# Fused attention and mixing on one Trainium2 core: where P is transposed in the first attention from the seventh pair on

## The chip, the core and the metric

The kernel runs on one core of one Trainium2 chip. The metric is the device time of one execution in microseconds (us). The engines are named as the profile names them: PE (TensorE), DVE (VectorE), ACT (ScalarE), POOL (GpSimd) and SP (SyncE, which only issues transfers here). PEld is PE's loading of weights, which runs beside its matmuls.

## What is computed

Three layers follow each other on 8 sequences of 576 tokens, with a width of 512. The change touches the first.

```python
# first attention: 8 heads of 64, in chunks of 64 tokens
scores = scale * q_c @ k_c.transpose(0, 1, 2, 4, 3)
attn = np.exp(scores - scores.max(-1, keepdims=True))
attn = attn / (attn.sum(-1, keepdims=True) + 1e-09)
x = attn @ v_c
# mixing: x_prev is x one token earlier
xk = mu_k * x + (1 - mu_k) * x_prev
xr = mu_r * x + (1 - mu_r) * x_prev
x = sigmoid(xr @ w_r) * (np.maximum(xk @ w_k, 0) ** 2 @ w_v)
# then four gated experts of causal attention, not touched here
```

## The kernel before, in words

Tokens are cut into 36 tiles of 128, two chunks of 64 each. Two tiles make a pair (18 pairs, 0 to 17), three tiles make a unit of the mixing layer (12 units of 384 tokens). The projections of the mixing layer are done with each operand split into a high and a low part, so that each product is three matmuls of 128x128 by 384 columns (`mm3`, L91 to L97).

The first attention of a pair runs in named steps. `lq`, `lk`, `lv` load a tile's queries, keys and values from SP (`load_qk`, `load_v`). `Tq` and `Tk` transpose queries and keys. From tile 12 on (`by_dve`, that is from the seventh pair) DVE does this in blocks of 32x32 (`by_blocks`, L197): the loads of such tiles place the blocks so that the transpose of each block alone is enough, in 8 transfers of 32 KB per tensor and tile (L149 to L153). Before tile 12, PE transposes whole 128x128 squares against an identity into a PSUM bank (`to_bank`, L187), and ACT copies the bank out in `Eq` and `Ek` (`from_bank`, L192). `S` makes the scores with 64 matmuls of 64x64 (`s_scores`, L211 or L214), into PSUM. On DVE `X` takes maxima and `U` subtracts them, on ACT `E` is the exponential, on DVE `Z` sums and inverts and `Y` multiplies: the result is P. `Tp` transposes P of one tile, in all pairs with four PE transposes (L187), and `Ep` copies the bank to the tile PT on ACT (L192). `V` multiplies PT by the values with 64 matmuls (`s_products`, L267 or L270) and `W` copies the results to XT.

The mixing steps: `a`, `b`, `c`, `d` (with `k` or `r`) shift and split x on ACT, DVE, ACT, DVE; `r`, `k` and each half of `v` are twelve matmuls on PE; `s` is the sigmoid, `K` three ACT steps (L364 to L366), `J` the low part on DVE (L370); `y` multiplies on DVE (L387), `z` takes the high part on POOL (L84), `x` the low part on DVE (L396), and `D` stores from POOL's queue (L401). `prev` moves a column on POOL.

The order of all this is written out by hand as two lists of steps: START for the first two units, with pairs 0 to 5 done in it, and TWO_UNITS, which is run four times (units 2 to 9, each turn with the attention of three pairs ahead: pairs 6 to 17). `follow` (L495) issues the steps in the list's order, and `in_line` (L485) chains each instruction to the one before on its own engine, so that every engine keeps the list's order. In TWO_UNITS the numbers are offsets: `Tp0` is the first tile of the turn, `V-1` the products of the pair that the turn before left over. After the fourth turn `V17` and `W17` stand alone (L515); the last two units and the experts follow in an order that the compiler's scheduler makes.

Attention's PSUM banks are five (`pa`), the tiles PT have two buffers, the tag `cz` (128x512) two, the loads two each.

Of the kernel before, what the change touches and what calls it, by code (L numbers as in the profile page):

```python
# [8 lines left out]
F32 = mybir.dt.float32  # L9
# [34 lines left out]
CH = 64  # L44
UNIT = 384
TWO_UNITS = """
Tk0 Tk1 lk2 Tq0 k0,0 Tq1 k0,1 K0,0 lq2 J0,0 V-1 S0 K0,1 k0,2 W-1 X0 U0 prev1 k0,3 ar1,0 K0,2 br1,0 J0,1 k0,4 E0 J0,2
lq3 K0,3 k0,5 J0,3 K0,4 Z0 k0,6 K0,5 lv0 J0,4 Y0 k0,7 K0,6 J0,5 J0,6 Tp0 K0,7 v0,0,0 lv1 lk3 cr1,0 J0,7 ar1,1 Tk2 Tp1
v0,0,1 dr1,0 Tq2 v0,1,0 y0,0 br1,1 z0,0 cr1,1 x0,0 v0,1,1 ak1,0 dr1,1 D0,0 bk1,0 ar1,2 lk4 br1,2 v0,2,0 cr1,2 ck1,0
dr1,2 y0,1 ak1,1 v0,2,1 z0,1 bk1,1 dk1,0 ck1,1 x0,1 ar1,3 v0,3,0 D0,1 y0,2 br1,3 z0,2 cr1,3 v0,3,1 dr1,3 dk1,1 ak1,2  # L50
Ep0 r1,0 y0,3 x0,2 z0,3 Tk3 D0,2 r1,1 bk1,2 s1,0 lk5 ak1,3 r1,2 ck1,2 bk1,3 dk1,2 ck1,3 Tq3 s1,1 r1,3 s1,2 lq4 dk1,3
Ep1 V0 S1 k1,0 W0 X1 x0,3 s1,3 k1,1 U1 D0,3 K1,0 lq5 J1,0 k1,2 K1,1 E1 J1,1 k1,3 lv2 K1,2 k1,4 Z1 K1,3 Y1 k1,5 J1,2
lv3 Tq4 K1,4 Tp2 J1,3 lq6 k1,6 Ep2 J1,4 K1,5 Tk4 k1,7 Tk5 K1,6 J1,5 Tq5 lk6 Tp3 J1,6 v1,0,0 Ep3 K1,7 V1 S2 J1,7 v1,0,1
X2 W1 U2 prev2 v1,1,0 ar2,0 lk7 br2,0 ar2,1 y1,0 cr2,0 br2,1 v1,1,1 z1,0 dr2,0 cr2,1 ar2,2 dr2,1 ar2,3 v1,2,0 y1,1 lv4
x1,0 z1,1 lq7 br2,2 D1,0 v1,2,1 br2,3 cr2,2 E2 x1,1 dr2,2 v1,3,0 Z2 ak2,0 cr2,3 lv5 D1,1 Y2 v1,3,1 dr2,3 bk2,0 ak2,1
Tp4 y1,2 ck2,0 r2,0 Ep4 z1,2 y1,3 dk2,0 z1,3 x1,2 Tp5 s2,0 x1,3 D1,2 r2,1 bk2,1 Ep5 r2,2 ck2,1 ak2,2 dk2,1 s2,1 bk2,2
ak2,3 D1,3 r2,3 ck2,2 bk2,3 s2,2 dk2,2 ck2,3 dk2,3 s2,3
""".split()

FIRST_UNITS, FIRST_PAIRS = 2, 6  # L60
CFG = dict(ps=(2, 3, 1, 2), P=5, sm=3, load=5, lag=(3, 4), out=(5, 1), qk1=(1, 1), qk0=(9, 1.1), v=(10, 0.9), order=((3, 0), (2, 0), (0, 0), (4, 0), (1, 0), (3, 1), (2, 1), (0, 1), (1, 1)), after=1, conv='v', clo='v', chi='g', x2hi='g', x2lo='v', ylo='g', yhi='v', xt='aa', r2='av', klo='vv', amul='vv', nearly=2, x2b=1, yb=4, qb=4, direct=((0, 1), (1, 1), (1, 1)), tailAV=4, kp=2, yt=1, yf=2, zb=1, om=(3, 2, 1, 0, 4), hp=1000, x2d=2, early=(2, 1), dact=3, rate0=0.43, rate=0.45, sh=(10, 12, 2), sh2=(11, 1, -1), pro='cccqqaacavvcaaaaacaacaaaascc', alag=2, seq=0, end=2, outL=(11, 2), outE=2, kcp='aa', dsc='v', ldb=2, vb=2, cn=512, stb=2, xb=4, pa=5, tb=2, first_j=7, dve_j=6)
# [38 lines left out]
def attn_mix(tc, at, x2T, q, k, v, mu_k, mu_r, w_k, w_v, w_r, ident, attended_all, mixed_k):  # L100

    nc = tc.nc
    B, H, S, D = q.shape
    HP = H // 2
# [10 lines left out]
    with ExitStack() as ctx:  # L115
# [15 lines left out]
        qkv = {}  # L131

        def runs(t):
            b, s = divmod(t * 128, S)
            return [(0, b, s, 128)] if s + 128 <= S else [(0, b, s, CH), (CH, b + 1, 0, CH)]

        def by_dve(t):
            return t >= 2 * CFG["dve_j"]
# [21 lines left out]
                qkv[nm, t] = x  # L160

        def load_v(t):
            if by_dve(t):
                x = at.tile([128, H, D], F32, tag="ldv", bufs=CFG["vb"], name="ldv")
                for p, b, s, n in runs(t):
                    nc.sync.dma_start(out=x[p:p + n], in_=v[b, :, s:s + n, :].rearrange("h p d -> p h d"))
                qkv["v", t] = x
                return
            x = at.tile([128, 2, HP, D], F32, tag="ldv", bufs=CFG["vb"], name="ldv")
            for c in range(2):  # L170
                b, s = divmod(t * 128 + c * CH, S)
                for e in range(2):
                    r = e ^ c
                    nc.sync.dma_start(out=x[r * 64:(r + 1) * 64, c],
                                      in_=v[b, e::2, s:s + CH, :].rearrange("g p d -> p g d"))
            qkv["v", t] = x

        qT, kT, PP, PT, XT = {}, {}, {}, {}, {}
# [11 lines left out]
        def from_bank(p, nm):  # L190
            o = at.tile([128, HP, 128], F32, tag=nm, bufs=CFG["tb"], name=nm)
            nc.scalar.activation(out=o, in_=p, func=ACTF.Copy)  # L192
            return o
# [6 lines left out]
        def s_scores(j):  # L200
            banks = [bank("Sps").rearrange("p g (i k) -> p i g k", i=2) for _ in range(2)]
            for i in range(2):
                a, b = qT.pop(2 * j + i), kT.pop(2 * j + i)
                for g in range(HP):
                    for c in range(2):
                        for o in range(2):
                            e = o ^ c
                            r, cc = slice(e * 64, e * 64 + 64), slice(c * CH, (c + 1) * CH)
                            with tc.high_priority(1000) if j < CFG["first_j"] else nullcontext():
                                if by_dve(2 * j):  # L210
                                    nc.tensor.matmul(out=banks[e][cc, i, g], lhsT=a[r, g, c], rhs=b[r, g, c],  # L211
                                                     start=True, stop=True)
                                    continue
                                nc.tensor.matmul(out=banks[o][cc, i, g], lhsT=a[r, g, cc], rhs=b[r, g, cc],  # L214
                                                 start=True, stop=True)
            SB[j] = banks
# [38 lines left out]
        def s_products(j):  # L255
            VB[j] = banks = [bank("PVps").rearrange("p g (i k) -> p i g k", i=2) for _ in range(2)]
            for i in range(2):
                t = 2 * j + i
                a, vt = PT.pop(t), qkv.pop(("v", t))
                for g in range(HP):  # L260
                    for c in range(2):
                        for o in range(2):
                            e = o ^ c
                            r, cc = slice(o * 64, o * 64 + 64), slice(c * CH, (c + 1) * CH)
                            with tc.high_priority(1000) if j < CFG["first_j"] else nullcontext():
                                if by_dve(t):
                                    nc.tensor.matmul(out=banks[o][cc, i, g], lhsT=vt[r, 2 * g + c],  # L267
                                                     rhs=a[r, g, cc], start=True, stop=True)
                                    continue
                                nc.tensor.matmul(out=banks[c][e * 64:e * 64 + 64, i, g], lhsT=vt[r, c, g],  # L270
                                                 rhs=a[r, g, cc], start=True, stop=True)

# [110 lines left out]
        X2 = {}  # L383
# [25 lines left out]
        n = CFG["cn"]  # L409
# [45 lines left out]
        def to_T(d, nm):  # L455
            def f(t):
                x = PP.pop(t).rearrange("p g o k -> p (g o k)") if nm == "PT" else qkv.pop((nm[0], t))
                if nm != "PT" and by_dve(t):
                    d[t] = by_blocks(x, nm)
                else:  # L460
                    TB[nm, t] = to_bank(x)
            return f

        def from_T(d, nm):
            def f(t):
                d[t] = from_bank(TB.pop((nm, t)), nm)
            return f

        TB = {}
        stages = dict(  # L470
            L=c_load, A=c_scale, G=c_bits, B=c_join, H=c_hi, O=c_lo,
            lq=lambda t: load_qk(t, "q"), lk=lambda t: load_qk(t, "k"), lv=load_v,
            Tq=to_T(qT, "qT"), Tk=to_T(kT, "kT"), Tp=to_T(PT, "PT"),
            Eq=from_T(qT, "qT"), Ek=from_T(kT, "kT"), Ep=from_T(PT, "PT"),
            S=s_scores, X=s_max, U=s_sub, E=s_exp, Z=s_sum, Y=s_mul, V=s_products, W=s_result,
            prev=s_prev, mu=one_less_mu, r=r_mm, s=r_sig, k=k_mm, K=k_act, J=k_lo,
            v=v_mm, y=v_mul, z=v_hi, x=v_lo, D=v_store)
# [16 lines left out]

        def follow(steps, unit=0, tiles=0):  # L495
            ahead = {}
            for x in ("lq", "lk", "lv", "Tq", "Tk", "Tp", "Eq", "Ek", "Ep"):
                ahead[x] = tiles
            for x in "SXUEZYVW":
                ahead[x] = tiles // 2  # L500
            for s in steps:
                nm = s.rstrip("-0123456789,")
                args = [int(x) for x in s[len(nm):].split(",") if x]
                if args:
                    args[0] += ahead.get(nm, unit)
                if nm in ("lq", "lk", "lv") and args[0] >= nT:
                    continue
                at0 = len(traced)
                stages[nm](*args)
                in_line(at0)  # L510
# [6 lines left out]
        for u in range(NU - 2, NU):  # L517
# [6 lines left out]
            for i, (f, *args) in enumerate(items):  # L524
# [6 lines left out]
                if u + 1 < NU:  # L531
                    if i == KD:
                        s_prev(u + 1)
                    for w, at1 in ((1, CFG["sh"][0]), (0, CFG["sh"][1])):
                        g, r = divmod(i - at1, CFG["sh"][2])
# [507 lines left out]
```

## Time and profile before

| | |
|---|---|
| median of 3 runs | 981.07 us (980.85 to 982.61) |
| the profiled execution | 981.03 us |
| its span, first to last instruction | 978.7 us |
| mean granted TensorE clock | 0.991 |
| busy: PE, DVE, ACT, POOL | 937.5, 662.0, 622.5, 206.0 us |

The profile is one execution. The span is 2.3 us shorter than the execution's own time; the rest lies around it. A queue marked with q (SPq, POOLq) holds what an engine's sequencer does, the issue of transfers among it. Matmuls overlap in PE's pipeline, so that what a matmul costs is the distance from its start to the next one's, not its duration.

### The profile page before, as it was taken

How to read it: one execution, taken by the hardware profiler on the slowest of the kernel's cores; microseconds unless marked ns; L12 is line 12 of the kernel's file. 1: busy time of each engine (PE TensorE's matmuls, PEld its weight loads, DVE VectorE, ACT ScalarE, POOL GpSimd, SP SyncE). 2: the span in 40 equal slices, each digit the busy share in tenths (PEclk: the TensorE clock that was granted, in tenths of full speed). 3: DMA queues.
4: the chain of work that ended last, by engine and by line, in shares of the span. 5: the costliest groups of instructions: out<-in, count | busy, mean ns of one | idle time of the engine just before them, and what ended most of it. 6: DMA issues, size and time to landing. Idle time of an engine off the chain costs nothing.

```text
span 978.7 us, 21549 instructions
## 1 busy us (share of the span) xinstructions
PE 937.5 (96%) x8022; PEld 904.4 (92%) x8022; DVE 662.0 (68%) x1625; ACT 622.5 (64%) x1417; POOL 206.0 (21%) x392
## 2 busy tenths in 40 slices
PE   2689999999999999999999999999999999999997
PEld 2589999999999999999999999898989998999995
DVE  7999746657565755575566612677877787778795
ACT  3598466665756574757576732667675677667684
POOL 3111111101120202020202115513333333323111
PEclk9799999999999999999999999999999999999999
DMA  9884433444324543444322217656362845445322
GB/s 250 203 197 127 87 84 81 86 87 98 83 67 91 114 72 73 81 108 73 77 68 80 59 47 160 135 138 184 68 187 67 211 73 169 123 136 142 99 55 88
DMA packets 223408, 108.39 MB, mean 111 GB/s; under 512 B 187352, under 2 KB 199752, under 8 KB 223304
## 3 DMA queue, kind: packets, MB, share of 16 engines
q1 hardware_dynamic: 193032, 67.16, 30.1%
q0 software_dynamic: 30272, 39.86, 15.5%
q8 instruction: 64, 1.05, 0.5%
q14 instruction: 40, 0.33, 0.1%
HBM read 66.01 MB, written 28.38 MB: 96 GB/s over the span
## 4 chain that ended last, share of the span: by engine, by line
PE 89%; DVE 5%; DMA 4%; issue 1%; ACT 1%; SPq 0%; POOL 0%; POOLq 0%; ACTq 0%; DVEq 0%
PE mps L95 17%; PE mps L96 17%; PE mps L97 17%; PE pj L95 7%; PE pj L96 6%; PE pj L97 6%; PE Sps L753 5%; PE Tps L806 4%; PE AVps L839 2%; PE AVps L835 2%; PE Tps L187 2%; DMA x<-x2T 2%; PE PVps L267 1%; PE Sps L211 1%; DMA ldq<-in_q_dram 1%; DMA st<-in_moe_w_v_dram 1%
## 5 line engine op out<-in xcount | busy, mean ns | idle before, releaser
L95 PE MATMUL mps<-xhk,wkh 128*128 128x384 f32 x384 | 130.7, 340 | 0.0
L95 PE MATMUL mps<-kh,wvh 128*128 128x384 f32 x384 | 129.6, 339 | 0.0
L96 PE MATMUL mps<-xlk,wkh 128*128 128x384 f32 x384 | 129.0, 336 | 0.0
L97 PE MATMUL mps<-xhk,wkl 128*128 128x384 f32 x384 | 129.0, 336 | 0.0
L96 PE MATMUL mps<-kl,wvh 128*128 128x384 f32 x384 | 128.5, 335 | 0.0
L97 PE MATMUL mps<-kh,wvl 128*128 128x384 f32 x384 | 128.4, 334 | 0.0
L370 DVE TENSOR_TENSOR kl<-r,kh 128x384 fp32r<-128x384 f32 x96 | 53.8, 561 | 87.4 <-ACT kh L366 86.8
L765 ACT ACTIVATE P<-sm,nm 128x512 f32<-128x512 f32 (+3 forms) x144 | 83.9, 584 | 22.1 <-DVE nm L755 15.6
L755 DVE CUSTOM_DVE_ANT_0 sm<-Sps,mask 128x256 f32<-128x256 f32 (+4 forms) x160 | 74.5, 477 | 29.5 <-PE Sps L753 28.7
L84 POOL CAST x2d<-x2o 128x384 fp32r<-128x384 f32 x48 | 33.5, 702 | 271.9 <-DVE x2o L387 268.5
L813 DVE TENSOR_TENSOR PTl<-Tps,PTh 128x512 fp32r<-128x512 f32 (+2 forms) x144 | 70.2, 505 | 4.9 <-ACT PTh L812 2.9
L95 PEld LDWEIGHTS mps<-xhk,wkh 128*128 128x128 f32 x384 | 72.2, 188 | 0.6
L95 PEld LDWEIGHTS mps<-kh,wvh 128*128 128x128 f32 x384 | 72.0, 188 | 0.4
L96 PEld LDWEIGHTS mps<-xlk,wkh 128*128 128x128 f32 x384 | 72.2, 188 | 0.0
L97 PEld LDWEIGHTS mps<-xhk,wkl 128*128 128x128 f32 x384 | 72.2, 188 | 0.0
L96 PEld LDWEIGHTS mps<-kl,wvh 128*128 128x128 f32 x384 | 72.1, 188 | 0.0
L97 PEld LDWEIGHTS mps<-kh,wvl 128*128 128x128 f32 x384 | 72.1, 188 | 0.0
L308 DVE SCALAR_TENSOR_TENSOR xa<-XT,mu,xa 128x384 f32<-128x384 f32 x96 | 60.3, 637 | 15.9 <-ACT xa L304 15.7
L364 ACT ACTIVATE r<-mps 128x384 f32<-128x384 f32 x96 | 46.4, 484 | 37.3 <-PE mps L97 37.2
L304 ACT ACTIVATE xa<-XT,mu 128x384 f32<-128x384 f32 x96 | 57.5, 614 | 18.6 <-DVE xlr L319 17.3
L812 ACT ACTIVATE PTh<-Tps 128x512 fp32r<-128x512 f32 (+2 forms) x144 | 61.6, 453 | 8.5 <-PE Tps L806 7.1
L806 PE MATMUL Tps<-ident,P 128*128 128x128 f32 x384 | 63.9, 274 | 2.7 <-DVE z L768 1.4
(183 smaller groups left out, 2629.3 us busy)
## 6 DMA issues: line engine op xcount, KB each, us to landing
x2T<-x2d POOLq DMA_DIRECT2D x48, 384.0 KB, 3.1
x<-x2T POOLq DMA_DIRECT2D x32, 576.0 KB, 6.5
K<-Kph SPq DMA_DIRECT2D x64, 128.0 KB
out_dram<-o SPq DMA_DIRECT2D x32, 256.0 KB
ldk<-in_k_dram SPq DMA_DIRECT2D x192, 32.0 KB
ldq<-in_q_dram SPq DMA_DIRECT2D x192, 32.0 KB
ldv<-in_v_dram SPq DMA_DIRECT2D x21, 256.0 KB
st<-in_moe_w_k_dram SPq DMA_DIRECT2D x8, 512.0 KB
```

What stands on the lines that cost most here:

```text
L95: nc.tensor.matmul(out=out, lhsT=ah, rhs=bh, start=first and i == 0, stop=False)
L96: nc.tensor.matmul(out=out, lhsT=ah, rhs=bl, start=False, stop=False)
L97: nc.tensor.matmul(out=out, lhsT=al, rhs=bh, start=False, stop=last and i == n - 1)
L304: nc.scalar.activation(out=a, in_=XT[u][:, g, :, :SEG], func=ACTF.Copy, scale=mu1[:, w, g:g + 1])
L308: nc.vector.scalar_tensor_tensor(a, XT[u][:, g, :, 1:], mu[:, w, g:g + 1], a, op0=ALU.mult, op1=ALU.add)
L370: eng(nc, CFG["klo"][u >= CFG["nearly"]]).tensor_tensor(o.lo, K2.pop((u, m)), f32(o.hi), op=ALU.subtract)
L753: issued = nc.tensor.matmul(out=pp[:, :w], lhsT=x, rhs=y[:, a:a + w], start=n == 0, stop=n == len(terms) - 1)
L755: nc.vector.tensor_tensor_reduce(out=sm[:, a:a + w], in0=pp[:, :w], in1=mk[:, :w], op0=ALU.add, op1=ALU.min, scale=-scale, scalar=3e38, ac ...
L765: nc.scalar.activation(out=x[:, :nk], in_=sm[:, :nk], func=ACTF.Exp, scale=-1.0, bias=nm[:, :1], accum_out=z)
L806: nc.tensor.transpose(pp[:, j], x[:, j * 128:(j + 1) * 128], ident)
L812: nc.scalar.activation(out=h, in_=src, func=ACTF.Copy)
L813: nc.vector.tensor_tensor(l, src, f32(h), op=ALU.subtract)
```

## The change

From tile 12 on, `Tp` becomes one DVE transpose of P by 32x32 blocks into a new tile of the tag `cz`. `Ep` becomes a POOL copy of that whole tile to PT. The blocks on the diagonal of each 64x64 square are then in place, those off it are not: a new step `Cp` (`cross`) issues four transfers from POOL's queue, each from 32 partitions of the transposed tile to 32 partitions of PT, 8 pieces of 128 B per partition (32 KB). The score matmuls write other partition halves of the two banks, so that heads and chunks lie as in the first pairs; the value loads (four transfers of 64 partitions) and the product matmuls of the first pairs are then used for all. TWO_UNITS is replaced by a new order that holds `Cp`; START stays.

```diff
-Tk0 Tk1 lk2 Tq0 k0,0 Tq1 k0,1 K0,0 lq2 J0,0 V-1 S0 K0,1 k0,2 W-1 X0 U0 prev1 k0,3 ar1,0 K0,2 br1,0 J0,1 k0,4 E0 J0,2
...
-Ep1 V0 S1 k1,0 W0 X1 x0,3 s1,3 k1,1 U1 D0,3 K1,0 lq5 J1,0 k1,2 K1,1 E1 J1,1 k1,3 lv2 K1,2 k1,4 Z1 K1,3 Y1 k1,5 J1,2
...
+Tq0 Tk0 lq2 Tq1 k0,0 Tk1 k0,1 K0,0 lk2 J0,0 V-1 S0 K0,1 k0,2 X0 W-1 J0,1 prev1 k0,3 U0 ar1,0 K0,2 k0,4 E0 J0,2 lk3
+K0,3 Z0 k0,5 K0,4 J0,3 k0,6 J0,4 K0,5 lq3 Y0 k0,7 Tp0 K0,6 J0,5 Ep0 Tk2 Cp0 J0,6 v0,0,0 K0,7 lv0 ak1,0 J0,7 Tq2 v0,0,1
+Tp1 lq4 bk1,0 Ep1 ck1,0 v0,1,0 dk1,0 Cp1 br1,0 ar1,1 cr1,0 br1,1 v0,1,1 dr1,0 cr1,1 lv1 Tq3 ar1,2 y0,0 v0,2,0 dr1,1
+z0,0 Tk3 ar1,3 x0,0 v0,2,1 br1,2 D0,0 br1,3 cr1,2 dr1,2 cr1,3 v0,3,0 ak1,1 dr1,3 y0,1 z0,1 y0,2 V0 S1 bk1,1 x0,1 ck1,1
+ak1,2 D0,1 v0,3,1 X1 lv2 z0,2 U1 r1,0 dk1,1 lv3 bk1,2 ak1,3 lq5 r1,1 E1 bk1,3 y0,3 s1,0 Z1 z0,3 r1,2 ck1,2 dk1,2 ck1,3
+s1,1 lk4 r1,3 dk1,3 x0,2 Y1 k1,0 s1,3 Tp2 s1,2 Ep2 k1,1 K1,0 Cp2 J1,0 k1,2 K1,1 Tq4 lk5 Tp3 D0,2 J1,1 Ep3 k1,3 K1,2 W0
+J1,2 Cp3 k1,4 K1,3 k1,5 J1,3 K1,4 Tq5 k1,6 J1,4 K1,5 Tk4 Tk5 lk6 k1,7 x0,3 K1,6 J1,5 J1,6 V1 S2 K1,7 J1,7 v1,0,0 W1 X2
...
+ak2,0 dr2,3 y1,2 ak2,1 bk2,0 r2,0 ck2,0 z1,2 y1,3 bk2,1 z1,3 Tp5 r2,1 x1,2 Ep5 s2,0 dk2,0 D1,2 Cp5 r2,2 ck2,1 ak2,2
+dk2,1 s2,1 bk2,2 ak2,3 x1,3 r2,3 ck2,2 bk2,3 s2,2 D1,3 dk2,2 ck2,3 dk2,3 s2,3
...
         def load_v(t):
-            if by_dve(t):
-                x = at.tile([128, H, D], F32, tag="ldv", bufs=CFG["vb"], name="ldv")
-                for p, b, s, n in runs(t):
-                    nc.sync.dma_start(out=x[p:p + n], in_=v[b, :, s:s + n, :].rearrange("h p d -> p h d"))
-                qkv["v", t] = x
-                return
...
                                 if by_dve(2 * j):
-                                    nc.tensor.matmul(out=banks[e][cc, i, g], lhsT=a[r, g, c], rhs=b[r, g, c],
-                                                     start=True, stop=True)
+                                    nc.tensor.matmul(out=banks[e][o * 64:o * 64 + 64, i, g], lhsT=a[r, g, c],
+                                                     rhs=b[r, g, c], start=True, stop=True)
...
-                                if by_dve(t):
-                                    nc.tensor.matmul(out=banks[o][cc, i, g], lhsT=vt[r, 2 * g + c],
-                                                     rhs=a[r, g, cc], start=True, stop=True)
-                                    continue
...
-                if nm != "PT" and by_dve(t):
+                if by_dve(t) and nm == "PT":
+                    TB[nm, t] = at.tile([128, H * CH], F32, tag="cz", bufs=2, name="Pb")
+                    nc.vector.transpose(TB[nm, t], x)
+                elif by_dve(t):
                     d[t] = by_blocks(x, nm)
...
-                d[t] = from_bank(TB.pop((nm, t)), nm)
+                if not by_dve(t):
+                    d[t] = from_bank(TB.pop((nm, t)), nm)
+                    return
+                x = TB[nm, t]
+                d[t] = o = at.tile([128, HP, 128], F32, tag=nm, bufs=CFG["tb"], name=nm)
+                nc.gpsimd.tensor_copy(o.rearrange("p g c -> p (g c)"), x)
             return f
+
+        def cross(t):
+            src = TB.pop(("PT", t)).rearrange("p (h w b) -> p h w b", w=2, b=32)
+            dst = PT[t].rearrange("p g (c w b) -> p (g c) w b", w=2, b=32)
+            for r in range(0, 128, 64):
+                for w in range(2):
+                    to, of = (slice(r + 32 * k, r + 32 * k + 32) for k in (w, 1 - w))
+                    nc.gpsimd.dma_start(out=dst[to, :, 1 - w], in_=src[of, :, w])
...
-            Eq=from_T(qT, "qT"), Ek=from_T(kT, "kT"), Ep=from_T(PT, "PT"),
+            Eq=from_T(qT, "qT"), Ek=from_T(kT, "kT"), Ep=from_T(PT, "PT"), Cp=cross,
```

## Rows read from the trace of the kernel before

**Rows 1.** The page: the span, and busy time by engine.
```profile
span 978.7 us, 21549 instructions
...
PE 937.5 (96%) x8022; PEld 904.4 (92%) x8022; DVE 662.0 (68%) x1625; ACT 622.5 (64%) x1417; POOL 206.0 (21%) x392
```
**Rows 2.** Busy by stretch: us, PE, PEld, DVE, ACT, POOL, clock, DMA share, GB/s.
```profile
299.60:391.90 92.30, 92.30 (x882) 91.16 (x876) 57.29 (x100) 58.80 (x111) 11.91 (x20) 1.00 0.42 87
```
**Rows 3.** Waits of PE's weight queue, 340 to 440 us: total, times, longest.
```profile
PEld PVps L267 <- issue: 0.8, 3, 0.2
```
**Rows 4.** Chain that ended last, 300 to 330 us: start, us, what.
```profile
313.35 0.44 PE Tps L187 x4
```
**Rows 5.** Timeline of PE about one group of P transposes: start, us, instructions.
```profile
224.65 0.34 PE L95 MATMUL mps<-xhk,wkh 128*128 128x384 f32 x1
...
224.99 0.34 PE L97 MATMUL mps<-xhk,wkl 128*128 128x384 f32 x1
225.17 0.60 PE L187 MATMUL Tps<-ident,P 128*128 128x128 f32 x4
225.52 0.43 PE L95 MATMUL mps<-kh,wvh 128*128 128x384 f32 x1
225.78 0.34 PE L96 MATMUL mps<-kl,wvh 128*128 128x384 f32 x1
```
**Rows 6.** Timeline of PE about two product sets, one of each arrangement.
```profile
165.35 1.16 PE L270 MATMUL PVps<-PT,ldv 64*64 64x64 f32 x64
166.34 1.11 PE L211 MATMUL Sps<-kT,qT 64*64 64x64 f32 x64
...
205.96 1.16 PE L267 MATMUL PVps<-PT,ldv 64*64 64x64 f32 x64
206.94 1.11 PE L211 MATMUL Sps<-kT,qT 64*64 64x64 f32 x64
```
**Rows 7.** Wait instructions on PE's weight queue at the product lines: ns min/median/max.
```profile
L270 PEldq EVENT_SEMAPHORE  x12: 51/51/51, 36.8 to 162.9; - x12
...
L267 PEldq EVENT_SEMAPHORE  x22: 51/51/51, 202.8 to 531.8; - x22
```
**Rows 8.** Groups of instructions by shape: busy us, mean ns, idle before.
```profile
L308 DVE SCALAR_TENSOR_TENSOR xa<-XT,mu,xa 128x384 f32<-128x384 f32 x96 | 60.3, 637 | 15.9 <-ACT xa L304 15.7
L370 DVE TENSOR_TENSOR kl<-r,kh 128x384 fp32r<-128x384 f32 x96 | 53.8, 561 | 87.4 <-ACT kh L366 86.8
L366 ACT ACTIVATE kh<-r 128x384 fp32r<-128x384 f32 x96 | 50.5, 526 | 2.8
L396 DVE TENSOR_TENSOR x2d<-x2o,x2d 128x384 fp32r<-128x384 f32 x48 | 27.7, 586 | 5.1 <-POOL x2d L84 4.9
L387 DVE TENSOR_TENSOR x2o<-mps,sig 128x384 f32<-128x384 f32 x48 | 26.5, 556 | 37.6 <-PE mps L97 36.6 <-ACT r L365 0.9
L248 DVE TENSOR_TENSOR P<-P,m 128x1024 f32<-128x1024 f32 x18 | 22.3, 1236 | 0.3
L197 DVE STREAM_TRANSPOSE kT<-ldk 128x512 f32<-128x512 f32 x24 | 16.0, 694 | 0.0
L84 POOL CAST wkh<-cz 128x512 fp32r<-128x512 f32 x8 | 7.0, 869 | 33.1 <-DVE cz L435 33.1
```
**Rows 9.** POOL's transfers: two lines' durations and landings, and four issues in a row.
```profile
L401 POOL DMA_DIRECT2D x2T<-x2d x29: 717/717/726, 210.4 to 525.4; - x29
...
DMA to landing us min/median/max: 2.8/3.2/5.4
...
DMA to landing us min/median/max: 4.2/6.5/10.1
...
780.19 2.99 POOL L673 DMA_DIRECT2D x<-x2T  x4 [14.19 <-PE Sps L753]
```
**Rows 10.** Timeline and durations of SP's issues of query and value loads.
```profile
205.03 5.29 SPq L151 DMA_DIRECT2D ldq<-in_q_dram  x9
...
L174 SPq DMA_DIRECT2D ldv<-in_v_dram x48: 596/614/1658, 26.0 to 139.9; - x48
```

More of the change, by code (lines that the diff above doesn't have):

```diff
@@ L46 @@
 TWO_UNITS = """
-Tk0 Tk1 lk2 Tq0 k0,0 Tq1 k0,1 K0,0 lq2 J0,0 V-1 S0 K0,1 k0,2 W-1 X0 U0 prev1 k0,3 ar1,0 K0,2 br1,0 J0,1 k0,4 E0 J0,2
[L48 to L51, printed above, removed]
@@ L52 @@
-Ep1 V0 S1 k1,0 W0 X1 x0,3 s1,3 k1,1 U1 D0,3 K1,0 lq5 J1,0 k1,2 K1,1 E1 J1,1 k1,3 lv2 K1,2 k1,4 Z1 K1,3 Y1 k1,5 J1,2
[L53 to L56, printed above, removed]
@@ L57 @@
-ak2,3 D1,3 r2,3 ck2,2 bk2,3 s2,2 dk2,2 ck2,3 dk2,3 s2,3
+Tq0 Tk0 lq2 Tq1 k0,0 Tk1 k0,1 K0,0 lk2 J0,0 V-1 S0 K0,1 k0,2 X0 W-1 J0,1 prev1 k0,3 U0 ar1,0 K0,2 k0,4 E0 J0,2 lk3
+K0,3 Z0 k0,5 K0,4 J0,3 k0,6 J0,4 K0,5 lq3 Y0 k0,7 Tp0 K0,6 J0,5 Ep0 Tk2 Cp0 J0,6 v0,0,0 K0,7 lv0 ak1,0 J0,7 Tq2 v0,0,1
+Tp1 lq4 bk1,0 Ep1 ck1,0 v0,1,0 dk1,0 Cp1 br1,0 ar1,1 cr1,0 br1,1 v0,1,1 dr1,0 cr1,1 lv1 Tq3 ar1,2 y0,0 v0,2,0 dr1,1
+z0,0 Tk3 ar1,3 x0,0 v0,2,1 br1,2 D0,0 br1,3 cr1,2 dr1,2 cr1,3 v0,3,0 ak1,1 dr1,3 y0,1 z0,1 y0,2 V0 S1 bk1,1 x0,1 ck1,1
@@ new lines @@
+ak1,2 D0,1 v0,3,1 X1 lv2 z0,2 U1 r1,0 dk1,1 lv3 bk1,2 ak1,3 lq5 r1,1 E1 bk1,3 y0,3 s1,0 Z1 z0,3 r1,2 ck1,2 dk1,2 ck1,3
+s1,1 lk4 r1,3 dk1,3 x0,2 Y1 k1,0 s1,3 Tp2 s1,2 Ep2 k1,1 K1,0 Cp2 J1,0 k1,2 K1,1 Tq4 lk5 Tp3 D0,2 J1,1 Ep3 k1,3 K1,2 W0
+J1,2 Cp3 k1,4 K1,3 k1,5 J1,3 K1,4 Tq5 k1,6 J1,4 K1,5 Tk4 Tk5 lk6 k1,7 x0,3 K1,6 J1,5 J1,6 V1 S2 K1,7 J1,7 v1,0,0 W1 X2
+lv4 lq6 U2 prev2 v1,0,1 D0,3 ar2,0 ar2,1 br2,0 cr2,0 br2,1 v1,1,0 E2 y1,0 dr2,0 z1,0 lv5 x1,0 v1,1,1 cr2,1 Z2 D1,0
+ar2,2 lq7 v1,2,0 y1,1 dr2,1 z1,1 ar2,3 x1,1 v1,2,1 Y2 D1,1 Tp4 v1,3,0 lk7 br2,2 Ep4 br2,3 cr2,2 Cp4 dr2,2 cr2,3 v1,3,1
@@ L496, in follow @@
             ahead = {}
-            for x in ("lq", "lk", "lv", "Tq", "Tk", "Tp", "Eq", "Ek", "Ep"):
+            for x in ("lq", "lk", "lv", "Tq", "Tk", "Tp", "Eq", "Ek", "Ep", "Cp"):
                 ahead[x] = tiles
```

## The prediction

> **What bounds the kernel now.** I read the engine totals first: the span is 978.7 us and PE is busy 96% of it, DVE 68%, ACT 64%, POOL 21% [rows 1]. The change touches only the attention of pairs 6 to 17, which runs inside the four turns of the written-out list, so the next view is busy time by stretch. In one turn, from 299.6 to 391.9 us, PE is busy for all 92.3 us at full granted clock, DVE for 57.3, ACT for 58.8, POOL for 11.9 [rows 2]. The waits say the same: in 100 us of that stage TensorE's queue waited 0.8 us in all, on its own issue, and on no engine and no transfer [rows 3]. The chain that ended last runs through every P transpose, 0.44 us for each group of four [rows 4]. So in this stage time is the sum of PE's work, and what leaves PE leaves the time, as long as nothing else arrives late.
>
> **What leaves PE.** Look at one group in PE's order [rows 5]: the projection matmuls start 0.173 us apart (224.65 to 225.17 is three of them), the last one before the group starts at 224.99, and the second one after it at 225.78. That is 0.79 us where two steps of 0.173 would do: a group costs 0.44 us, the same as in the chain. The matmul list has six such groups per turn and four turns, 24 in all: 24 x 0.44 = **10.5 us off PE**. ScalarE loses its 24 copies out of PSUM, off the path.
>
> **What is regrouped.** Score and product matmuls change which quarter of the PSUM partitions they write, so neighbours now differ in rows and columns. The products of the first pairs already have that arrangement: 64 of them hold PE from 165.35 to 166.34, 0.99 us; those of a later pair, in the old arrangement, from 205.96 to 206.94, 0.98 us [rows 6]. I take nothing, bounds 0.01 us a pair either way.
>
> **What the products now wait for.** A product set waits for eight crossing transfers where it waited for two ScalarE copies, and for eight value loads where it waited for two or three. A separate wait instruction takes PE's weight queue 51 ns; the first six product sets, with eight loads each, have 12 of them, the later twelve have 22 [rows 7]. If each of the eight new transfers took one: 12 x 8 x 0.051 = 4.9 us lost; if all 22 went away, 1.1 us won. I take 0, because in rows 6 the set with eight loads is no longer than the one with fewer.
>
> **What DVE and POOL gain.** DVE gets 24 transposes; the same operation on a same-sized tile takes 0.69 us, so 4.2 us a turn, 61.5 of about 90. POOL gets, per tile, a copy of 128x512, for which the nearest row is a cast of that size, 0.87 us, and four issues. The nearest issues are of POOL's own transfers: 0.72 us each in this stage, and 2.99 us for four in a row with 512 pieces each, twice a crossing's 256 [rows 8, 9]. So 0.87 + 2.99 = 3.9 us a tile, 23 a turn, POOL 35 of 90. No engine comes near PE in amount; lateness is the question.
>
> **Whether the products find their P.** PE works in steps of twelve matmuls, 12 x 0.173 = 2.09 us (a k, an r, or half a v). The tightest place is the third pair. Count from the end of v1,3,1. DVE does y1,3 (0.56), bk2,1 (0.64) and Tp5 (0.69), with hops 2.0 us [rows 8]. POOL then does Ep5 (0.87), D1,2 (0.72; it waits for x1,2, 0.59 on DVE, done by 2.6) and three issues (2.25): the last issue starts at 5.9. POOL transfers of this stage land 3.2 us after the start of issue at the median, 2.8 to 5.4 [rows 9], so the last quarter is there at 9.1. PE has r2,0 to r2,3, k0,0 and k0,1 before the products: six steps, 12.5 us. Cover left: 3.4 us.
> In the first pair Tp1 comes after J0,7, which needs K0,7 (three ScalarE steps near 0.53) and 0.56 of its own, then Tq2 and Tp1: 3.5 us after k0,7 with hops. The products are seven steps away, 14.6. With 0.87 and 2.25 the last issue starts at 6.6: 8.0 us for its landing. In the second pair Tp3 ends some 5.7 us after k1,0 starts (k1,0 itself, K1,0, J1,0, Tq4, Tp3), D0,2 costs 0.6 ahead of Ep3, the products are eight steps away, 16.7: 7.3 us for landing. In the third it is 12.5 - 5.9 = 6.6. Median and longest row both fit, so the first eleven product sets cost nothing.
> The exception is the end of the list: the products of pair 17 follow r2,3 directly, with no k0,0 and k0,1 in front: PE is there at 4 x 2.09 = 8.4, the data at 9.1. **Stall 0.7 us, once** (0.3 at the shortest landing, 2.9 at the longest).
>
> **Loads.** The value loads are four issues per tile instead of one or two, on SP: some 17 more a turn at 0.61 us, 10 us. SP issues nine query loads in 5.3 us [rows 10], 16 a tile and six tiles make 57 us of a turn, so it still ends inside 90. The place with the least room is `lv1`: it stands behind lq4's eight issues (4.7 us), which wait until Tq2 has emptied their buffer, some 2.8 us after k0,7. Its last issue then starts at 2.8 + 4.7 + 3 x 0.61 = 9.3, and the second tile's products at 15.1: 5.8 us for its landing. No view shows landings of SP's transfers; POOL's 2.8 to 5.4 fit. Cost 0; a longer landing holds one product set a turn by what it is over.
>
> **The sum.** The profiled execution took 981.03 us, 0.04 under the median of 981.07, so they count as one: 981.03 - 10.5 + 0.7 = **971.2 us**. Own range: 970 (shortest landing, PE waits saved) to 976 (all eight waits paid at full price).
>
> **A rule against it.** The rows show POOL's 29 issues of this stage at 717 to 726 ns, whatever DVE did, with DVE busy 62% of the time [rows 2, 9]. The Trainium skill's page "SBUF — State Buffer", section "SBUF: two separate sides", says that VectorE can lock GpSimd out of their common port while it writes descriptors, so that a transfer issued there of 620 ns takes some 3100 ns beside a VectorE copy. By the rows four issues cost 2.99 us; by that figure, as an estimate, 4 x 3.1 = 12.4 us a tile, some 19 us more a pair against covers of 4, or about 1150 us in all. The rows side against it as long as DVE's new instructions behave like its present ones.
>
> **Rivals.**
> 1. *PE pays the waits.* All as forecast, but every product set pays its wait instructions, or small shifts of order cost a few tenths a pair: up to 12 x 0.4 = 4.9, **976 us**. For it: rows 7 show such instructions exist. Against: rows 6.
> 2. *Landing too late (slower).* The crossings are 1024 pieces of 128 B a tile and share the DMA engines with SP's loads. The place is each product set; covers from the last issue are 8.0, 7.3, 6.6 and, at the end, 2.5 us. At a landing of L the stalls are 4(L-8.0) + 4(L-7.3) + 3(L-6.6) + (L-2.5), positive parts only: they eat the 10.5 us at L = 7.8. The longest landing of a large POOL load is 10.1 us [rows 9]: 8.4 + 11.2 + 10.5 + 7.6 = 38, **1008 us**. Against: the stage's longest is 5.4, for transfers of 384 KB against 32.
> 3. *POOL held at issue (slower).* If each issue had to wait out one DVE instruction, the longest in the stage being 1.24 us [rows 8], an issue is 2.0 us. A tile's four take 8 us, the first tile's run some 4 us into the second's, and the last issue then starts about 7.8 us later: against covers left of 4.8, 4.1 and 3.4 that is about 3.7 us a pair, 12 x 3.7 = 44, **1015 us**. This is the mechanism of the rule above. Against: the 726 ns.
> 4. *PE was not what bounds* (the change does not bring what it removes): relieved of 10.5 us, PE waits as much for DVE or ACT in the new order, **981 us**. For it: DVE has queues of ten instructions that no view prices one by one. Against: rows 2 and 3, with 35 us of DVE idle per turn.
> 5. *More than counted*: the new order also removes the small gaps before product sets and helps the part after the list, **968 us**.
>
> **How the numbers follow.** Forecast 0.64, rival 1 0.15, rival 2 0.06, rival 3 0.04, rival 4 0.06, rival 5 0.05. A measurement of this kernel can tell about 0.2%, 2 us, from no change. Faster is the forecast with rivals 1 and 5: 0.84; no change is rival 4 but for a hundredth: 0.05; slower is rivals 2 and 3 and that hundredth: 0.11. The range runs from 968 (rival 5) to 976 (rival 1 and the price of the waits); outside lie rivals 2, 3 and 4, 0.16, and the ends of 1 and 5, some 0.03.
>
> **What would show it.** Right: no P transpose on PE between 170 and 530 us, PE still 100% busy there, a turn shorter by six groups, 2.6 us, the DVE transposes near 0.69, the four issues near 3.0 us, landings of 3 to 5 us, one wait of under 3 us before the last products. Wrong: PE waiting for the crossings before each product set (rival 2 if landings are long, rival 3 if issues are), or for DVE in front of k or r (rival 4); copies on POOL well over 0.87 us would eat cover first in the third pair.

## The result and the profile after

The kernel after the change takes 968.91 us (median of 4 runs, 967.97 to 970.70), the kernel before beside it 981.21 (980.85 to 982.61): a ratio of 0.988 [0.987, 0.989], 12.3 us faster. A second measurement of both gave 969.56 (968.55 to 970.68) beside 980.35, ratio 0.989 [0.988, 0.991], and the kernel before once more 980.65, ratio 1.0005 [0.999, 1.001]. The profiled execution of the changed kernel took 967.97 us at a mean granted clock of 0.996.

The page of the kernel after, to be laid beside [rows 1]:

```profile
span 966.2 us, 21715 instructions
...
PE 926.8 (96%) x7926; PEld 894.8 (93%) x7926; DVE 678.2 (70%) x1649; ACT 611.6 (63%) x1393; POOL 276.2 (29%) x512
```

PE has lost 10.7 us and 96 instructions (24 tiles of four transposes). DVE has gained 16.2 us, POOL 70.2 us and 120 instructions, which are 24 copies and 96 issues; ACT has lost 10.9.

One turn of the list now runs from 255.7 to 345.8 us. Busy time in that stretch (us; PE, PEld, DVE, ACT, POOL, clock, DMA share, GB/s), as in [rows 2]:

```profile
255.70:345.80 90.10, 90.10 (x868) 89.15 (x872) 61.00 (x107) 55.94 (x105) 30.00 (x51) 1.00 0.46 97
```

The turn is 90.10 us long, and PE is busy for all of it, as before. DVE's 61.0 is what the prediction added up (61.5), POOL's 30.0 is less than its 35.

The waits of PE's weight queue in the same 100 us as [rows 3]:

```profile
PEld PVps L260 <- issue: 1.0, 4, 0.2
```

No wait for a crossing, for DVE or for POOL: 1.0 us, on PE's own issue, where 0.8 stood.

The new instructions of the kernel after, by line (durations in ns, min/median/max, with first and last start): the DVE transpose, the POOL copy, the four transfers with their landing, and the separate wait instructions at the product line.

```profile
L450 DVE STREAM_TRANSPOSE Pb<-P x24: 668/708/712, 178.8 to 514.5; 128x512 f32<-128x512 f32 x24
...
L464 POOL COPY PT<-Pb x24: 613/794/855, 179.6 to 515.4; 128x512 f32<-128x512 f32 x24
...
L473 POOL DMA_DIRECT2D PT<-Pb x96: 582/585/619, 180.7 to 518.6; - x96
...
DMA to landing us min/median/max: 1.8/2.1/4.5
...
L260 PEldq EVENT_SEMAPHORE  x96: 51/51/51, 35.7 to 522.2; - x96
```

The transposes are as forecast (0.69), the copies a little shorter (0.87 was taken), the issues and the landings shorter than their nearest rows by a fifth and a third: 0.585 against 0.75, 2.1 us against 3.2. Of the 96 wait instructions 12 belong to the first six product sets, as in [rows 7]. So 84 stand at the twelve changed sets, seven a set, where 22 stood.

Where the time came from is read from three landmarks in the chain of waits: pair 5's products (ahead of the first changed turn), pair 17's (behind the last), and the last output copy. Before (start, us, what):

```profile
165.43 1.09 PE PVps L270 x64
...
531.72 1.09 PE PVps L267 x64
...
974.30 0.60 ACT o L879
```

After:

```profile
165.68 1.09 PE PVps L260 x64
...
521.83 1.15 PE PVps L260 x62
...
962.50 0.60 ACT o L885
```

From pair 5 to pair 17 the kernel before needs 366.29 us, the one after 356.15: **10.14 us gained**. In the second pair of executions these two distances are 366.30 and 356.16, once more 10.14. From pair 17 to the last output copy it is 442.58 before and 440.67 after, 1.91 less; but in the second pair of executions it is 440.75 and 440.71, so that part doesn't come back. The first execution of the kernel before lost it at two places. At one it waited on a late load of the experts, which its chain shows and the chain of the kernel after does not:

```profile
674.43 10.07 DMA x<-x2T
```

Not all of the 10.07 us is lost: the output copies on either side, which start at 681.30 and 727.76 us, are only 0.92 us further apart than in the second execution of the same kernel (682.80 and 728.34). The other place is near the end, where the granted clock (third number from the end; columns as in [rows 2]) of the first execution, in the first row, is lower than that of the second:

```profile
957.00:966.00 9.00, 7.68 (x43) 5.96 (x42) 6.67 (x20) 4.93 (x15) 2.98 (x3) 0.81 0.20 71
...
955.00:970.00 15.00, 12.62 (x76) 9.93 (x75) 10.95 (x38) 7.69 (x22) 3.00 (x3) 1.00 0.16 55
```

Two output copies about this place are 11.51 us apart in the first (957.57 and 969.08) and 10.69 in the second (958.12 and 968.81), 0.82 less.

Behind the last output copy something does come back. From its start to the end of the span it is 4.4 us in both executions of the kernel before, and 3.7 and 3.6 in those of the kernel after. In the runs below it is 4.4 to 4.5 wherever the value loads and the arrangement of heads and chunks are those of before, and 3.6 to 3.7 wherever they are the new ones. So **0.7 us** at the end belong to the change too.

So the two profiled executions differ by 13.06 us: 10.14 in the four turns, 1.91 behind them, and 1.01 in the start, behind the last copy and around the span. The 10.14 and the 0.7 at the end are the same each time, 10.8 us together; the others changed from one execution of the same kernel to the next. The medians lie 12.3 and 10.8 us apart. For the second execution of the kernel after, a turn of 90.1 us and 444 to 447 us from pair 17 to the end of the span were expected; it has 90.11 and 444.4, as the first (447.0 and 445.1 before). The rival, a gain of some 2.5 us behind the list, had 444.4 as well, but a median under 969; measured are 969.56, and 0.7 us less than the second execution of the kernel before.

### The profile page after: what moved, and what is told of

It reads as the page before. It is cut to its first block, busy times and chain, and to the rows that moved or that the text cites. A ratio compares the mean times of both kernels' runs of the same rounds, so it can differ in the third digit from the quotient of the medians.

```text
span 966.2 us, 21715 instructions
## 1 busy us (share of the span) xinstructions
PE 926.8 (96%) x7926; PEld 894.8 (93%) x7926; DVE 678.2 (70%) x1649; ACT 611.6 (63%) x1393; POOL 276.2 (29%) x512
## 4 chain that ended last, share of the span: by engine, by line
PE 90%; DVE 5%; DMA 3%; ACT 1%; issue 1%; SPq 0%; ACTq 0%; DVEq 0%
PE mps L95 17%; PE mps L97 17%; PE mps L96 17%; PE pj L95 7%; PE pj L96 7%; PE pj L97 7%; PE Sps L759 5%; PE Tps L812 4%; PE AVps L845 2%; PE AVps L841 2%; PE PVps L260 2%; PE Sps L205 1%; DMA st<-in_moe_w_v_dram 1%; DVE PTl L819 1%; DMA st<-in_moe_w_r_dram 1%; DVE sm L761 1%
## 5 line engine op out<-in xcount | busy, mean ns | idle before, releaser
L819 DVE TENSOR_TENSOR PTl<-Tps,PTh 128x512 fp32r<-128x512 f32 (+2 forms) x144 | 70.2, 505 | 4.8 <-ACT PTh L818 2.9
L84 POOL CAST x2d<-x2o 128x384 fp32r<-128x384 f32 x48 | 30.9, 647 | 122.7 <-DVE x2o L377 121.1
```

The costliest lines, as they stand in the source:

```text
L819: nc.vector.tensor_tensor(l, src, f32(h), op=ALU.subtract)
```

## The experiments

The theory: in the turns the time is the sum of PE's work; the transposes leave it, the crossings find room in the new order, and nothing else is gained. The rivals: the order of the list brings the gain by itself; the products' waits or the crossings cost PE something that is hidden in the sum; the old order would have carried the crossings as well.

**The new list alone.** The kernel before with the new TWO_UNITS, its `CpN` left out, and P still transposed on PE.

```diff
-Tk0 Tk1 lk2 Tq0 k0,0 Tq1 k0,1 K0,0 lq2 J0,0 V-1 S0 K0,1 k0,2 W-1 X0 U0 prev1 ...
+Tq0 Tk0 lq2 Tq1 k0,0 Tk1 k0,1 K0,0 lk2 J0,0 V-1 S0 K0,1 k0,2 X0 W-1 J0,1 prev1 ...
...
-Ep0 r1,0 y0,3 x0,2 z0,3 Tk3 D0,2 ...
+K0,3 Z0 k0,5 K0,4 J0,3 k0,6 J0,4 K0,5 lq3 Y0 k0,7 Tp0 K0,6 J0,5 Ep0 Tk2 J0,6 v0,0,0 ...
```

> The kernel before with the new list of two units (its Cp steps left out); P is transposed by PE as before. Theory (PE's work sets the time, and the change gained by taking 24 groups of 0.44 us off PE): the same work on PE, so the time of the kernel before, 981 us, within 1.5. Rival (the new order itself gained most of the 12.3 us): 969 to 974 us. Third possibility: in an order made for other engines PE waits for P at its transposes; then over 984 us.

Measured: 980.76 us, ratio 0.9999 [0.999, 1.001]. A turn, between the starts of its first product sets, is 92.57 us, where the kernel before has 92.61. One of its six groups of P transposes, in the chain of waits:

```profile
273.35 0.44 PE Tps L187 x4
```

The order brings nothing by itself; PE still pays 0.44 us per group. What the order is for, the next run shows.

**The change with the old list.** The kernel after, with the list of before; each `EpN` is followed by its `CpN`.

```diff
-K0,3 Z0 k0,5 K0,4 J0,3 k0,6 J0,4 K0,5 lq3 Y0 k0,7 Tp0 K0,6 J0,5 Ep0 Tk2 Cp0 J0,6 v0,0,0 ...
+lq3 K0,3 k0,5 J0,3 K0,4 Z0 k0,6 K0,5 lv0 J0,4 Y0 k0,7 K0,6 J0,5 J0,6 Tp0 K0,7 v0,0,0 ...
...
+Ep0 Cp0 r1,0 y0,3 x0,2 z0,3 Tk3 D0,2 ...
```

> The kernel after with the old list, each Cp set directly behind its Ep. Theory (the new operations hide only as far as the list keeps PE work between them and the products): first and third pair of a turn still hide, 6 and more us of PE work stand after their last transfer. In the second pair Tp3 is done some 1.4 us after k1,7, the copy and four issues of 0.58 us put the last issue near 4.0, landing 2.1 us later at 6.1, and the products stand at 2.1: a stall of about 4 us, once a turn, 16 us in all: 981.2 - 12.3 + 16 = 985 us, 980 to 989. Rival (transfers are hidden wherever they stand, the list does not matter): 969 us.

Measured: 992.7 us, ratio 1.0125 [1.010, 1.015]: slower than the kernel before, and 7.7 us over the expectation. The place was right: the second pair of each turn, where PE has only one half of a v between `Tp3` and `V1`. The chain of waits goes around through POOL and a landing there:

```profile
319.64 0.81 POOL PT L464
320.45 0.28 issue
320.73 0.58 POOL PT L473
321.32 2.40 DMA PT<-Pb
323.72 0.25 issue
323.96 0.30 PE PVps L260 x2
```

The copy of the pair's second tile, the first of its four issues and the landing of that one take 0.81, 0.58 and 2.40 us. PE meanwhile, in its timeline:

```profile
321.11 0.69 PE L260 MATMUL PVps<-PT,ldv 64*64 64x64 f32 x32
323.96 0.30 PE L260 MATMUL PVps<-PT,ldv 64*64 64x64 f32 x2 [2.16 <-DMA PT<-Pb]
324.85 1.02 PE L260 MATMUL PVps<-PT,ldv 64*64 64x64 f32 x27 [0.58 <-issue]
```

Half of the product set is done at its place, then PE is idle for 2.16 us, and for 0.58 once more within the rest. From this set's first matmul to the next pair's it is 33.97 us (355.08 less 321.11). The kernel before has 30.15 there (its chain has the two sets at 320.50 and 350.65), 29.27 less two groups of transposes: the set loses 4.7 us, where 4 were expected. The two waits are 2.7 of it. Behind them the granted clock is at half, 1.2 GHz, for 3.4 us (columns as in [rows 2]):

```profile
324.60:328.00 3.40, 3.15 (x95) 3.07 (x96) 0.27 (x1) 2.03 (x6) 0.00 (x0) 0.50 0.36 56
```

PE is busy for 3.15 us of that, half of which, 1.6 us, is lost; the expectation had no such term. The other two pairs of the turn lose 0.3 us at most. That makes this turn 94.74 us, 4.64 over the kernel after; the turns of this run are 94.1 to 96.1 us, and from pair 5's products to pair 17's it is 375.2 us, 19.0 over the kernel after, where 16 were expected. The rest of the miss was forgotten in the estimate: pair 17's products wait too, in three pieces with 0.36 and 0.61 us of idle time between them, and from their start to the last output copy it is 444.50 us, 3.8 more than in the kernel after. What of this lies behind the waits was not followed up. Under the old order the change loses more than the transposes bring.

**Without the crossings.** The kernel after with the four transfers left out. The copy on POOL stays.

```diff
-                    nc.gpsimd.dma_start(out=dst[to, :, 1 - w], in_=src[of, :, w])
+                    pass
```

> The kernel after without the crossing transfers: the off-diagonal blocks of P stay untransposed in place, so the products are of wrong weights. Theory (the transfers are hidden, products pay only some wait instructions, 5 more of 51 ns a set of which about 0.05 us shows): 968.3 us, between 967 and 969. Rival (transfers still hold up products or the DMA queues): 965 or less.

Measured: 968.6 us, ratio 0.9875 [0.986, 0.989], within the spread of the kernel after. The turn tells more than the total: 89.90 us, 0.20 less than the kernel after. The product line has 48 wait instructions here, 36 of them at the twelve changed sets, three a set. One product set and the score set behind it on PE, in this kernel:

```profile
348.67 1.16 PE L260 MATMUL PVps<-PT,ldv 64*64 64x64 f32 x64
349.65 1.11 PE L205 MATMUL Sps<-kT,qT 64*64 64x64 f32 x64
350.70 0.45 PE L95 MATMUL mps<-xhk,wkh 128*128 128x384 f32 x1
```

and the same place in the kernel after (the products' last two matmuls come among the scores there):

```profile
345.72 1.18 PE L260 MATMUL PVps<-PT,ldv 64*64 64x64 f32 x62
...
347.80 0.45 PE L95 MATMUL mps<-xhk,wkh 128*128 128x384 f32 x1
```

From the start of the products to the matmul behind the scores it is 2.03 us here, 2.08 in the kernel after, and 2.02 in the kernel before (its set of [rows 6], to the matmul at 207.98). By the turns, all that the crossings cost PE is 0.20 us a turn, 0.07 a product set, **0.8 us** in twelve (0.68 between the products of pair 5 and pair 17, which holds eleven of them). Four wait instructions more a set at 51 ns would be 0.20 a set; two thirds of them lie beside PE's work.

**The transposes twice on PE.** The kernel before, with the four PE transposes of P issued twice into the same bank from tile 12 on.

```diff
-            for g in range(HP):
+            for g in list(range(HP)) * times:
...
-                    TB[nm, t] = to_bank(x)
+                    TB[nm, t] = to_bank(x, 2 if by_dve(t) else 1)
```

> The kernel before with each P transposed twice on PE from tile 12 on, into the same bank. Four more transposes are 0.35 us by the timeline (0.44 with the change to and from them): theory 24 x 0.35 = 8.4 us more, 989.3 us, up to 991.5 with 0.44. Rival (transposes lie beside other waits and cost little): 983 or less; if a group truly cost 12.3 / 24 = 0.51 us, 993.

Measured: 990.9 us, ratio 1.0092 [1.008, 1.011]: 9.75 us over the 981.15 of the kernel before, 0.41 a group. A turn is 95.22 us, 2.61 more than before. The chain has each doubled group in it:

```profile
276.16 0.87 PE Tps L187 x8
277.03 0.18 PE mps L95
```

0.87 us for eight, 0.435 for four. Adding a group costs what taking one away brings, so PE's amount is what sets the length of a turn, on both sides of the kernel before.

**The old arrangement of heads and chunks.** The kernel after, with the value loads and the matmuls' partition halves of before, which mix heads and chunks in the results; only this is put back.

```diff
+            if by_dve(t):
+                x = at.tile([128, H, D], F32, tag="ldv", bufs=CFG["vb"], name="ldv")
...
-                                    nc.tensor.matmul(out=banks[e][o * 64:o * 64 + 64, i, g], lhsT=a[r, g, c],
+                                    nc.tensor.matmul(out=banks[e][cc, i, g], lhsT=a[r, g, c],
```

> The kernel after with the score and product matmuls in the arrangement of before and the value loads of before (one or two transfers a tile): heads and chunks are then mixed up in the products. Theory (regrouping and loads cost nothing): within 1 us of after, 968 to 970. Rival (four value loads a tile add waits that PE pays, up to 51 ns each): 966 or less; rival (the new arrangement lets matmuls overlap more): over 972.

Measured: 970.73 us (968.05 to 971.68), ratio 0.9881 [0.986, 0.990]. A turn is 90.09 us, 0.01 from the kernel after. In the turns, regrouping and the extra value loads cost and bring nothing. The median is 0.7 us above what was expected, and the piece behind the last output copy is 4.4 us long here, 0.7 more than in the kernel after: that piece hangs on the loads or on the arrangement, and this run put both back, so which of the two it is stays open.

**The crossings twice, issue by issue.** Each of the four transfers is issued twice in a row.

```diff
                     nc.gpsimd.dma_start(out=dst[to, :, 1 - w], in_=src[of, :, w])
+                    nc.gpsimd.dma_start(out=dst[to, :, 1 - w], in_=src[of, :, w])
```

> The kernel after with every crossing transfer issued twice. By the trace of after the last transfer of a pair lands (2.1 us after its issue) 5.9, 6.2 and 5.0 us ahead of the products of the three pairs of a turn, and 1.0 ahead of the last products (pair 17). Theory: four more issues of 0.58 us per tile use up to 3.3 us of that: nothing in the turns, and one stall of about 2.3 us before the products of pair 17: 971.2 us, 970 to 973. Rival (the transfers stand near their limit in every pair): 10 us and more, over 979.

Measured: 1138.75 us, ratio 1.1615 [1.160, 1.163], and it does not measure what it was meant to. The second transfer writes the blocks of the first, so POOL waits for the first one's landing ahead of every second issue, as POOL's timeline shows,

```profile
313.92 0.60 POOL L473 DMA_DIRECT2D PT<-Pb  x1 [0.30 <-POOL PT L464]
316.09 0.58 POOL L474 DMA_DIRECT2D PT<-Pb  x1 [1.57 <-DMA PT<-Pb]
```

and its waits, over the whole execution (total, times, longest):

```profile
POOL PT L474 <- DMA PT<-Pb: 178.0, 96, 3.4
```

That is 1.85 us a wait, and POOL's other work, `z` and `D` for PE's next steps, stands behind it. The run shows what a serial form of the crossing would cost, with the mean granted clock down at 0.927 in it. The change's four transfers write different blocks and wait for none of each other.

**A second pass, behind the first.** The same doubling in another order: all four crossings, then all four again, so that the repetition finds the first ones mostly landed.

```diff
-            for r in range(0, 128, 64):
+            for r in list(range(0, 128, 64)) * 2:
```

> The kernel after with the four crossing transfers of a tile issued a second time, after all four have been issued once, so that a repeated transfer finds its first copy landed (1.9 us after issue, while its own issue comes 2.33 us after). This puts right e4, where each repetition waited for the landing of the one just before it. Theory: as said there, 3.3 us of the 5.0 to 6.2 us of cover go in each pair, and only the products of pair 17 wait, about 2.3 us: 971 us, 969 to 973. Rival (the cover read from the trace is not there): over 979.

Measured: 975.57 us, ratio 0.9932 [0.991, 0.995], 6 to 7 us over the kernel after, where 2 were expected. Its turns are 90.0 to 90.8 us, up to 0.7 longer; from pair 5's products to pair 17's it is 357.25 us, 1.1 more than in the kernel after. Pair 17's products, the place with least cover, now come in pieces:

```profile
523.74 0.69 PE L260 MATMUL PVps<-PT,ldv 64*64 64x64 f32 x32
525.73 0.30 PE L260 MATMUL PVps<-PT,ldv 64*64 64x64 f32 x2 [1.29 <-DMA PT<-Pb]
526.65 0.78 PE L260 MATMUL PVps<-PT,ldv 64*64 64x64 f32 x30 [0.62 <-DMA PT<-Pb]
```

1.29 and 0.62 us of waiting for the crossings, where the kernel after has none. Behind them the granted clock is at half for 3.4 us, with PE busy all the time, which costs 1.7 us more:

```profile
527.11:530.51 3.40, 3.40 (x25) 3.29 (x17) 0.59 (x2) 1.24 (x4) 0.19 (x1) 0.50 0.61 150
```

From the start of these products to the last output copy it is 446.2 us, 5.5 more than in the kernel after; 3.6 of them are the waits and the clock, the other 1.9 have no place yet. POOL waited 16.0 us, in 21 waits, for the first pass to land, which the expectation had left out; that these waits are what the turns lose was not tried by itself.

**A third pass.** The same with three.

```diff
-            for r in range(0, 128, 64):
+            for r in list(range(0, 128, 64)) * 3:
```

> The same with three passes. Theory: POOL spends 7.0 us on a tile's issues, the last transfer lands 1.7 to 2.9 us after the products of each pair stand ready on PE, and 7 us after those of pair 17: 4 x (2.4 + 1.7) + 3 x 2.9 + 7.1 = 32 us, 1001 us, 990 to 1010. Rival (transfers never hold the products): 969 us.

Measured: 1040.62 us, ratio 1.0593 [1.056, 1.062]. The longest turn is 109.4 us, 19.3 longer than in the kernel after, where 7 were expected; from pair 5's products to pair 17's it is 417.2 us, 61 more. Now the crossings are late. The waits of PE's weight queue in that turn, 339.0 to 448.4 us:

```profile
PEld PVps L260 <- issue: 6.3, 6, 3.7
PEld PVps L260 <- POOL x2d L84: 3.7, 1, 3.7
PEld PVps L260 <- POOL XT L286: 2.2, 1, 2.2
PEld PVps L260 <- DMA PT<-Pb: 1.9, 2, 1.0
```

These are 14.1 us of waits of the product sets, part of them beside PE's work. The chain of waits about one of them, between 364 and 378 us, goes through a copy on POOL and three landings, one behind the other:

```profile
364.23 0.89 POOL PT L464
...
365.79 2.41 DMA PT<-Pb
...
369.35 3.77 DMA PT<-Pb
...
374.56 2.52 DMA PT<-Pb
...
377.12 1.01 PE PVps L260 x27
```

So each pass also waits for the one before. The rest of the turn's loss is for the most part the clock. The turn, and the stretch behind the set above:

```profile
339.02:448.40 109.38, 97.24 (x864) 95.07 (x865) 61.18 (x106) 55.93 (x105) 56.72 (x98) 0.94 0.46 98
377.20:380.58 3.38, 3.38 (x96) 3.26 (x97) 0.58 (x1) 1.76 (x4) 0.00 (x0) 0.50 0.69 127
```

PE stood for 12.1 us of the turn. At half the granted clock it worked for 12.5 us, 3.4 of them from 377.2 us, as many from 339.6 and 5.7 from 411.3, and half of that, 6.2, is lost. The two make 18.3 of the 19.3 us. The expectation, 32 us against the 71.7 measured, had neither the waits of one pass for another nor the clock. The direction bears on the change: with twice the issues the four turns together lose 1.1 us, with three times 61, so the cover is there and is not large.

## Why the prediction was right

The forecast was 971.2 us in a range of 968 to 976; measured were 968.9 and 969.6.

- **What leaves PE**, 24 groups at 0.44 us, 10.5 in all: right. The doubled transposes give 0.41 to 0.435 a group, and a turn without the crossings is 2.71 us shorter than before, 0.45 a group. The new list with the transposes left on PE is no faster, so the gain is theirs.
- **Regrouping and value loads** at nothing: right in the turns, 0.01 us each. The 0.7 us behind the last output copy, which hang on them, were in no term.
- **The products' waits** at nothing, bounds 4.9 lost and 1.1 won: mis-sized, 0.8 us lost. There are 62 more wait instructions. At 51 ns they would be 3.2 us, and most of them lie beside PE's work. I compared two sets of [rows 6] whose wait instructions hardly differ in number (two a set against 1.8) and took that for the price of seven. Rival 1, with 4.9 us, is out.
- **The stall of 0.7 us at pair 17**: wrong, there is none. The terms that failed are the issue, 0.75 taken and 0.585 measured, and the landing, 3.2 taken and 2.1 measured: I used the rows of larger transfers. POOL's timeline of the kernel after shows the last tile's copy and its four issues,

```profile
515.37 0.79 POOL L464 COPY PT<-Pb 128x512 f32<-128x512 f32 x1 [0.38 <-issue]
...
516.83 2.33 POOL L473 DMA_DIRECT2D PT<-Pb  x4
```

  the last of which starts a quarter before the end of the row, at 518.58; with 2.1 us for landing the data are there at 520.7. PE comes to them at 521.76, behind the last step of r, and its products are one piece:

```profile
521.49 0.34 PE L97 MATMUL mps<-xhr,wrl 128*128 128x384 f32 x1
521.76 1.22 PE L260 MATMUL PVps<-PT,ldv 64*64 64x64 f32 x64
522.91 0.44 PE L95 MATMUL mps<-xhk,wkh 128*128 128x384 f32 x1
```

  That is 1.0 us of cover where the sum had a lack of 0.7. In the three pairs of a turn the same reckoning gives 5.9, 6.2 and 5.0 us left (last issues at 276.93, 306.03 and 338.60; products at 284.96, 314.3 and 345.72), where 4.8, 4.1 and 3.4 were forecast: the same error of some 1 to 2 us, and the third pair the tightest as forecast.
- **The sum.** 10.8 off PE, by the run without the crossings, less 0.7 to 0.8 for the waits makes the 10.14 measured between the landmarks twice; but both figures come from the same run. The doubled transposes, 10.4, less the waits give 9.6 to 9.7, so that some 0.5 us is open; the new list alone, 366.13 us between the landmarks where the kernel before has 366.29, has 0.16 of it. The forecast's 10.5 less 0.7 came out at 9.8 by two errors that nearly cancel, waits that were left out and a stall that did not come: that the sum is so near is luck, the 10.5 is not. (A step of twelve matmuls is 2.08 us, not 2.09; no cover moves by more than about 0.1 us for it.) The remaining 2 us between 971.2 and the 969 measured lie for the most part outside the turns: 0.7 behind the last output copy, the rest in the parts that the landmarks show to vary; the profiled execution I subtracted from held a late load and a stretch of lower clock. Rival 5, 968 us, is nearest to the measured time, but its mechanism is seen only in small: the new order alone brings nothing, and the part behind the list is shorter only by the 0.7 us at its end, which do not come from the order, since the new list alone has 4.5 us there.
- **Rivals 2 and 3**, late landings and held issues: out. The longest landing was 4.5 us, the longest issue 619 ns, with DVE busy 61 of 90 us. By the rule of the Trainium skill, page "SBUF — State Buffer", section "SBUF: two separate sides", a transfer from GpSimd's queue that takes some 620 ns alone takes some 3100 ns beside a VectorE copy. None of the 96 issues shows such a time, so the rule did not bite on this mix of instructions; whether any of VectorE's instructions here is of the kind that the page means, no run shows. How near the cover was to its end is what the second and third pass show.
- **Rival 4**, PE not the bound: out, by the doubled transposes as much as by the change.

## What to carry to other kernels

Where the waits of the busiest engine's queue are nearly nothing over a whole stage, that stage's time is the engine's sum, and what leaves it leaves the time at its price in the chain; but the detour needs a place in the order, and the same change under the old order was slower than no change. Count the room from the last issue to the consumer for every pair, the end of the list too, since the place without the usual steps in front has the least. And time an edit between landmarks on either side of it: two executions of the kernel before differed by 1.8 us between the last two landmarks for reasons that lay elsewhere. A stall is to be priced with the clock behind it: where the crossings came late, PE lost the waits and then some microseconds at half the granted clock.

## What was not expected of the hardware

- A transfer of 32 KB between two places of the on-chip memory, in 256 pieces of 128 B, takes POOL 0.585 us to issue and lands 2.1 us after (1.8 to 4.5), against 0.72 and 3.2 for the stores of 384 KB in [rows 9].
- Two transfers to the same blocks, one behind the other on POOL's queue, cost a wait for the first landing each time in this program, 1.85 us in the mean of 96.
- A product set with four more wait instructions is only 0.07 us longer, where each takes PE's weight queue 51 ns.
- A wait of PE can cost more than its own length. In the run of three passes 12.1 us of standing still in a turn went with 6.2 us lost at a granted clock of 0.50; in the turns of the kernels before and after, where PE does not stand, it is 1.00.
- The last part of the kernel varies by some 2 us from one execution to another: a second load of the experts, behind one of some 5 us, stands in the chain for 10.07 us in the first profiled execution of the kernel before, for 9.24 in the run without the crossings, and not at all in the second execution of either kernel. What it costs is much less, 0.92 us in the first of these; another 0.82 went with a granted clock of 0.81 near the end.
